# A wait of GpSimd for VectorE's bf16 operations in a transformer block whose order is written out

## The chip, the cores and the metric

The kernel runs on one core of a Trainium2 chip (trn2). A core has five engines that run their own instruction streams: TensorE (PE, matmuls into PSUM), VectorE (DVE), ScalarE (ACT), GpSimd (POOL) and SyncE (SP, which issues DMAs here). They share the on-chip memory SBUF and meet only at semaphores. The metric is the device time of one execution in microseconds; lower is better.

## The reference

One block of a transformer with adaptive normalization, in bf16, for 2048 tokens of width 640. `c` gives, through `silu(c) @ w_mod`, six rows of 640: shift, scale and gate for each half of the block.

```python
h = _layernorm(x) * (1 + ca) + sa
x = x + ga * _A_ref(h, A_wqkv, A_wo)      # attention
h = _layernorm(x) * (1 + cb) + sb
x = x + gb * _B_ref(h, ...)               # down(sigmoid(h @ w_gate) * (h @ w_up))
```

The attention has 32 heads of 20 channels. A token sees itself and the 255 tokens before it (a band of width 256): scores outside the band are masked, then softmax, the sum over values, and the projection `wo`. The feed-forward part has 1536 hidden channels.

## The kernel before, in words

The tokens go in 8 chunks of 256 (`CH`), a chunk as two blocks of 128 rows. Each chunk passes these stages:

- `ln1`, `ln_stats`: VectorE takes the statistics of each row (L766, L768), GpSimd adds the epsilon and raises to the power -0.5 (L771, L773), and VectorE, or for six blocks GpSimd, normalizes the row (`x<-x,st`: L786 on VectorE, L783 on GpSimd). The block is then transposed by TensorE or by a DMA (L793), and `modulate` applies scale and shift to each of its five tiles of 128 channels (L802; on VectorE, ScalarE or GpSimd).
- `qkv`: matmuls with `wqkv` (L679), evacuation from PSUM (L878 on VectorE).
- `attention`: two halves of four head groups. For each, `score_set` puts scores into PSUM (`S`, L680), ScalarE takes the exponential into a buffer `E` (L988), and GpSimd cuts the edges of the band with `affine_select` (`masks`, L1013: three masks for each group, two of 512 elements per row and one of 1024). Then a *burst* of 64 or 32 matmuls multiplies all four `E` with the values (`burst`, L680, `M<-E,V`); it waits for every mask of its half. `norm` transposes the result out of PSUM (L1057, `T<-M`), takes reciprocals (L1062), divides (L1064, `Tn<-T,Dr`) and transposes back (L1066), all on VectorE. DMAs carry the result through DRAM.
- `outproj`: matmuls with `wo` and the residual sum on VectorE (L1118), then the second normalization and modulation, into `h2T`.
- `mlp`: matmuls with `wg`, `wu` (L679), the gate by tanh on ScalarE (L1163) and a product on VectorE (L1165), the down projection with `wd`, the second residual sum (L1184), and the store.

The gates of the two halves are multiplied into the weights once: rows of `wo` (L1207) and `wd` (L1146). The twelve rows of `wd` are done ten on VectorE, two on GpSimd; the rows are 128 partitions by 640 bf16.

What sets the order is a list. Every operation of the program is made by `Prog.op`, and gets its place from `PRIO`, a list of 2126 numbers written out in the kernel: the number is the place in the order, and its remainder by 5 is the engine. `schedule` walks through the operations in that order and estimates a start time for each, from its dependencies, from its engine's last end (less a constant, `OVERLAP`) and from when a buffer comes free; with it, it chooses which buffer of a pool a tile gets. `emit` then writes each engine's stream, with semaphore waits for an operation's dependencies only. A wait that the engine has already made, or that a later count covers, is left out.

Some VectorE operations are marked `port=True`: normalization (L786), modulation (L802), the division (L1064), the gate multiplies (L1146, L1207) and two tiny ones (L731), 76 on VectorE in all. In `schedule`, a marked VectorE operation is taken to start after the GpSimd operation ahead of it, and a GpSimd operation after the marked VectorE operation ahead of it (`portend`). In the program before, no instruction enforces that: it is part of the estimate alone. `PORTLAG = 0.05` is defined in the kernel and not used there.

Of the kernel before, what the change touches and what calls it, by code (L numbers as in the profile page):

```python
# [81 lines left out]
class Prog:  # L82
# [70 lines left out]
    def schedule(self):  # L153


        free = {e: START for e in ENGS}
# [7 lines left out]
        portend = 0.0  # L164
# [3 lines left out]
        def slot_time(pool, s):  # L168
            ten = pool.tenant[s]
            if ten is None:  # L170
                if not all(x.done for x in pool.init[s]):
                    return None
                return max([x.end + x.lat for x in pool.init[s]], default=0.0)
            return None if ten.left else freed[ten]
# [4 lines left out]
        def reached(x):  # L179
            for lo, n, s, d in reversed(past):  # L180
                if lo < x:
                    return s + d * (x - lo) / n
            return -100.0

        def take(t, s):
            ten = t.pool.tenant[s]
            t.prev = list(t.pool.init[s]) if ten is None else list(ten.rel)
            t.slot = s
            t.pool.tenant[s] = t

        for o in sorted(self.ops, key=lambda x: x.prio):
            assert all(d.done for d in o.deps), o.tag
            e = ENGS[o.prio % 5]
            assert e in o.engs, (o.tag, e)
            o.eng = e
            st = max([o.tmin, free[e] + (SWITCH if e == "pe" and o.mode != pemode else 0.0)]
                     + [d.end + (0.0 if d.eng == "pe" and e == "pe" and d is not o.fence else d.lat) for d in o.deps])
            if o.isdma and e == "sp":
                st = max(st, bw - QMAX)
            for t in o.tiles:  # L200
                if t.slot is None:
                    step = 1 if t.mate is None else 2
                    best = None
                    for s in range(0, len(t.pool.tenant), step):
                        rts = [slot_time(t.pool, s + k) for k in range(step)]
                        if None not in rts and (best is None or max(rts) < best[0]):
                            best = (max(rts), s)
                    assert best is not None, (o.tag, t.name)
                    if t.mate is None:
                        take(t, best[1])  # L210
                    else:
                        take(t, best[1] + t.odd)
                        take(t.mate, best[1] + 1 - t.odd)
                for x in t.prev:
                    st = max(st, x.end + x.lat)
            if e == "dve" and o.port:
                st = max(st, free["pool"])
            elif e == "pool":
                st = max(st, portend)
                if o.part != part:  # L220
                    st = max(st, free[e] + OVERLAP[e] + 0.06)
                part = o.part
            dur = o.dur[e]
            if e == "pe":
                st = max(st, reached(count - RING) + FETCH, reached(count + o.ni - RING) + FETCH - dur)
                past.append((count, max(o.ni, 1), st, dur))
                count += max(o.ni, 1)
                pemode = o.mout
            o.start = st
            free[e] = st + dur - OVERLAP[e]  # L230
            if e == "dve" and o.port:
                portend = free[e]
            if o.isdma:
                turn = o.dlat > 3.0
                if e == "sp" and bw - st > 2.0:
                    free[e] += 0.35 if o.dur[e] > 1.0 else 0.1
                own = st + o.dlat + 2.0 * o.work
                bw = max(st + o.dlat, bw + (MIXED if turn != lastturn and bw > st + o.dlat else 0.0)) + o.work
                lastturn = turn
                o.end = max((own if e == "act" and own < bw else bw) - 0.83, st + dur)  # L240
                s = rr
                rr = (rr + 1) % NDMA
                dmacnt[s] += 16
                o.key, o.val = f"d{s}", dmacnt[s]
                if dmalast[s] is not None:
                    o.deps.append(dmalast[s])
                dmalast[s] = o
            else:
                o.end = st + dur
            order[e].append(o)  # L250
            o.done = True
            for t in o.tiles:
                t.left -= 1
                if t.left == 0:
                    last = {}
                    for x in t.ops:
                        if x.isdma:
                            last[x] = x
                    for e2 in ENGS:
                        xs = [x for x in t.ops if x.eng == e2 and not x.isdma]  # L260
                        if xs:
                            last[e2] = max(xs, key=lambda x: x.start)
                    t.rel = list(last.values())
                    freed[t] = max(x.end + x.lat for x in t.rel)
# [3 lines left out]
    def emit(self):  # L268
        nc = self.nc
        pos = {}  # L270
        for e in ENGS:
            for i, o in enumerate(self.order[e]):
                pos[o] = i
        need = {}
        for e in ENGS:
            for o in self.order[e]:
                ds = list(o.deps)
                for t in o.tiles:
                    ds.extend(t.prev)
                ws = []  # L280
                for d in ds:
                    if d is o:
                        continue
                    if d.eng == e and not d.isdma:
                        assert pos[d] < pos[o], (d.tag, o.tag)
                        if e in ("pe", "sp") and d is not o.fence:
                            continue
                    ws.append(d)
                    d.signal = True
                need[o] = ws  # L290
        for p, o in zip(self.order["pool"], self.order["pool"][1:]):
            if p.part != o.part and p not in need[o]:
                need[o].append(p)
                p.signal = True
        for e in ENGS:
            cnt = 0
            for o in self.order[e]:
                if o.isdma:
                    continue
                if o.signal:  # L300
                    cnt += 1
                    o.key, o.val = e, cnt
        handles = {}

        def h(k):
            if k not in handles:
                handles[k] = nc.alloc_semaphore(f"sem_{k}")
            return handles[k]

        finals = {}  # L310
        for o in self.order["sp"] + self.order["act"]:
            if o.isdma and o.tag == "out":
                finals[o.key] = max(finals.get(o.key, 0), o.val)
        with nc.Block() as block:
            for e in ENGS:
                ops = self.order[e]
                if not ops:
                    continue

                def body(engine, ops=ops, e=e):  # L320
                    seen = {}
                    for o in ops:
                        w = {}
                        for d in need[o]:
                            if seen.get(d.key, 0) < d.val and w.get(d.key, 0) < d.val:
                                w[d.key] = d.val
                        for k, v in w.items():
                            engine.wait_ge(h(k), v)
                            seen[k] = v
                        ins = o.fn(engine, e)  # L330
                        if o.isdma:
                            ins.then_inc(h(o.key), 16)
                        elif o.signal:
                            ins.then_inc(h(o.key), 1)
                    if e == "sp":
                        for k, v in finals.items():
                            if seen.get(k, 0) < v:
                                engine.wait_ge(h(k), v)

                getattr(block, ENGATTR[e])(body)  # L340
# [142 lines left out]
PORTLAG = 0.05  # L483
# [776 lines left out]
```

## Time and profile before

| what | value |
| --- | --- |
| time before, median of 3 runs | 329.09 us (328.69 to 329.17) |
| the profiled execution's own time | 329.38 us |
| its span in the profile | 327.6 us |
| granted TensorE clock | 1.00 |
| operations in the list: TensorE, ScalarE, VectorE, GpSimd, SyncE | 920, 331, 420, 255, 200 |

Times in the profile's views count from the start of the span. A row of a timeline gives the start, the length, the engine, the line of the kernel, the operation, the tiles it writes and reads (`out<-in`), the shapes, how many neighbouring operations are merged (`x4`), and in brackets the idle time of the engine ahead of it with what ended that time. A row of the waits gives the waiting engine, tile and line, then what it waited for, the sum in us, how often, and the longest. Engine busy time includes time in which an operation is held up after its start.

### The profile page before, as it was taken

The page shows a single profiled execution, that of the slowest core. Times are in us where ns is not written, and L with a number is a line of the kernel's source. Part 1 is how long each engine was busy: PE and PEld are TensorE (multiplying, and loading weights), DVE is VectorE, ACT ScalarE, POOL GpSimd, SP SyncE. Part 2 cuts the span into 40 slices and gives each one's busy share as a digit, 9 for nine tenths or more (in the row PEclk, how much of TensorE's full clock was granted, in tenths as well). Part 3 has the DMA queues.
Part 4 walks back from the last instruction along what each step waited for, and adds up shares of the span by engine and source line. Part 5 has one row for each costly group of instructions (what it writes and reads, how often), then busy time and mean ns, then how long its engine had stood idle before and what let it go on. Part 6 is the DMA issues. An engine that isn't in the chain of part 4 may idle for free.

```text
span 327.6 us, 11602 instructions
## 1 busy us (share of the span) xinstructions
PE 318.1 (97%) x4878; PEld 222.8 (68%) x4879; DVE 216.9 (66%) x420; ACT 216.3 (66%) x322; POOL 184.0 (56%) x267
## 2 busy tenths in 40 slices
PE   8899899999988999999999999999999999999997
PEld 3665555556765568766876467877787788877885
DVE  3799987898799894786575465746545576563332
ACT  2598787887756678977778886867679765112220
POOL 4228768868949495767385857573758383011000
PEclk9999999999999999999999999999999999999999
DMA  7989689779951339613422654320311003303001
GB/s 258 368 269 376 139 190 165 143 195 333 226 117 38 62 73 129 109 43 97 120 54 57 113 89 109 91 69 4 85 49 48 27 11 88 101 7 76 28 22 40
DMA packets 71038, 37.85 MB, mean 116 GB/s; under 512 B 45258, under 2 KB 69066, under 8 KB 70986
## 3 DMA queue, kind: packets, MB, share of 16 engines
q1 hardware_dynamic: 69680, 35.64, 45.2%
q10 hardware_dynamic: 1306, 1.48, 1.4%
q8 instruction: 38, 0.62, 0.8%
q14 instruction: 14, 0.11, 0.1%
HBM read 21.30 MB, written 5.25 MB: 81 GB/s over the span
## 4 chain that ended last, share of the span: by engine, by line
PE 83%; DVE 9%; issue 3%; ACT 1%; DMA 1%; POOL 1%; ACTq 0%; DVEq 0%
PE M L679 70%; PE S L680 7%; PE M L680 6%; DVE wd L1146 2%; DMA x<-in_A_x_dram 1%; DVE Tn L1064 1%; ACT E L988 1%; DVE stg L878 1%; DVE T L1057 1%; DVE x L786 1%; DVE h2T L802 1%; DVE On L1066 1%; POOL E L1013 1%; DVE st L766 1%; POOL st L773 0%
## 5 line engine op out<-in xcount | busy, mean ns | idle before, releaser
L1013 POOL TENSOR_SCALAR_AFFINE_SELECT E<-E 128x512 bf16<-128x512 bf16 (+1 forms) x176 | 143.8, 844 | 69.2 <-ACT E L988 66.6
L988 ACT ACTIVATE E<-S 128x512 bf16<-128x512 f32 (+2 forms) x184 | 150.2, 877 | 42.7 <-PE S L680 38.7
L679 PE MATMUL M<-wqkv,hT 128*128 128x480 bf16 (+1 forms) x340 | 71.5, 355 | 0.9 <-DVE hT L802 0.6
L679 PE MATMUL M<-h2T,wg 128*128 128x256 bf16 x480 | 64.4, 273 | 0.7 <-DVE h2T L802 0.7
L679 PE MATMUL M<-h2T,wu 128*128 128x256 bf16 x480 | 63.6, 273 | 1.1 <-DVE T L1057 1.1
L679 PE MATMUL M<-wd,hh 128*128 128x320 bf16 (+2 forms) x396 | 57.3, 295 | 1.5 <-DVE x L1118 1.2
L1165 DVE SCALAR_TENSOR_TENSOR hh<-sig,M 128x512 bf16<-128x512 f32 x48 | 32.0, 678 | 38.3 <-ACT sig L1163 29.1
L1163 ACT ACTIVATE sig<-M 128x512 f32<-128x512 f32 x48 | 28.7, 599 | 41.0 <-PE M L679 32.8
L679 PEld LDWEIGHTS M<-h2T,wg 128*128 128x128 bf16 x480 | 45.5, 98 | 8.6 <-DVE h2T L802 1.1
L679 PEld LDWEIGHTS M<-h2T,wu 128*128 128x128 bf16 x480 | 45.1, 98 | 8.7 <-DVE T L1057 1.4
L679 PEld LDWEIGHTS M<-wqkv,hT 128*128 128x128 bf16 x340 | 30.9, 98 | 28.2 <-issue 1.3
L679 PEld LDWEIGHTS M<-wd,hh 128*128 128x128 bf16 x396 | 37.0, 98 | 15.9 <-DVE x L1118 1.6
L1184 DVE TENSOR_TENSOR x<-M,x 128x320 bf16<-128x320 f32 (+2 forms) x33 | 15.3, 475 | 28.5 <-PE M L679 28.3
L680 PEld LDWEIGHTS S<-QT,KT 20*64 20x64 bf16 (+1 forms) x1856 | 20.0, 100 | 20.7 <-issue 9.4
L680 PE MATMUL S<-QT,KT 20*64 20x256 bf16 (+5 forms) x1856 | 32.3, 228 | 0.8 <-issue 0.8
L766 DVE BATCH_NORM_STATS2 st<-x 128x6 f32<-128x320 bf16 x64 | 28.7, 479 | 3.1 <-DMA x<-in_A_x_dram 2.7
L771 POOL TENSOR_SCALAR st<-st 128x2 f32<-128x2 f32 x16 | 3.9, 241 | 39.5 <-DVE st L768 39.3
L1057 DVE STREAM_TRANSPOSE T<-M 128x512 f32<-128x512 f32 x32 | 21.0, 693 | 6.7 <-PE M L680 6.5
L679 PE MATMUL M<-wo,oT 128*128 128x320 bf16 x160 | 24.9, 299 | 0.0
L680 PE MATMUL M<-E,V 128*32 128x128 bf16 (+1 forms) x960 | 22.8, 246 | 0.4 <-DVE shB L731 0.3
L680 PEld LDWEIGHTS M<-E,V 128*32 128x32 bf16 x960 | 19.0, 97 | 4.6 <-POOL E L1013 2.2
L786 DVE TENSOR_SCALAR x<-x,st 128x640 bf16<-128x640 bf16 x26 | 14.4, 581 | 9.9 <-POOL st L773 9.9
(75 smaller groups left out, 250.1 us busy)
## 6 DMA issues: line engine op xcount, KB each, us to landing
x<-in_A_x_dram SPq DMA_DIRECT2D x21, 160.0 KB, 3.9
doc<-On SPq DMA_DIRECT2D x64, 40.0 KB
wd<-in_B_w_down_dram SPq DMA_DIRECT2D x4, 480.0 KB, 5.6
out_dram<-x SPq DMA_DIRECT2D x11, 160.0 KB, 1.8
wd<-in_w_mod_dram SPq DMA_DIRECT2D x5, 320.0 KB
wqkv<-in_A_wqkv_dram SPq DMA_DIRECT2D x4, 400.0 KB, 7.5
wu<-in_w_mod_dram SPq DMA_DIRECT2D x5, 320.0 KB
oT<-doc SPq DMA_DIRECT2D x8, 192.0 KB, 2.4
```

Of the source, the lines that this page charges most:

```text
L679: return e.matmul(o, l, r, start=st, stop=sp, skip_group_check=True)
L680: return e.matmul(o, l, r, start=st, stop=sp, tile_position=tp, skip_group_check=True)
L766: A("dve", lambda e, g, bi=bi, j=j: e.bn_stats(v(bi * 12 + j * 6, 6), src[bi].ap[:, j * 320:(j + 1) * 320]), 0.48, reads=[src[bi].r()], wr ...
L771: A("pool", lambda e, g: e.tensor_scalar(v(28, n), var(), EPS, None, op0=ALU.add), 0.2, reads=[st.r(("m", bi)) for bi in range(n)], writes ...
L786: return e.tensor_scalar(dst[bi].ap[:], src[bi].ap[:], v(24 + 2 * bi, 1), v(30 + bi, 1), op0=ALU.subtract, op1=ALU.mult)
L988: A("act", lambda e, eng: e.activation(dst(), src(), ACT.Exp, scale=SM_SCALE), c_act(n), reads=[Sp.r()], writes=[E.r(key)], prio=3, tag=f" ...
L1013: A("pool", lambda e, eng: e.affine_select(rows(dst), rows(src), pattern=[[0, 8], [sign, n]], compare_op=ALU.is_ge, fill=0.0, base=base, c ...
L1057: A("dve", lambda e, g, h=h: e.transpose(T1.ap[:, 512 * h:512 * h + 512], X[h].ap), 0.694, reads=[X[h].r()], writes=[T1.r(h)], prio=3.5, t ...
L1146: A(WSE[1], lambda e, g, t=t: e.tensor_tensor(wd[:, t, :], wd[:, t, :], gbc[:], op=ALU.mult), WS, port=True, reads=[R_wd[t // 3], R_gbc], ...
L1163: A("act", lambda e, g, pg=pg, sg=sg: e.activation(sg.ap[:], pg.ap[:], ACT.Tanh, scale=0.5), c_act(512), reads=[pg.r()], writes=[sg.r()], ...
L1165: A("dve", lambda e, g, pu=pu, sg=sg, f0=f0: e.scalar_tensor_tensor(out=hh.ap[:, f0:f0 + 2, :], in0=sg.ap[:].rearrange("p (a b) -> p a b", ...
L1184: A("dve", lambda e, g, ps=ps, bi=bi, c0=c0, n=n: e.tensor_tensor(x1[bi].ap[:, c0:c0 + n], ps.ap[:, 0:n], x1[bi].ap[:, c0:c0 + n], op=ALU. ...
```

## The change

`emit` gets one more loop. It goes through VectorE's and GpSimd's operations together in planned order, remembers the last marked VectorE operation, and makes each GpSimd operation wait for that one's end. VectorE does not wait for GpSimd in return. In `schedule`, the estimate of when a GpSimd operation may start after a marked one becomes its end plus `PORTLAG`, where it was its end less `OVERLAP` (0.075 for VectorE). The list is the same, so order and engine of every operation are.

```diff
@@ schedule
             if e == "dve" and o.port:
-                portend = free[e]
+                portend = st + dur + PORTLAG
@@ emit
                     ws.append(d)
                     d.signal = True
                 need[o] = ws
+        held = None
+        for o in sorted(self.order["dve"] + self.order["pool"], key=lambda x: x.prio):
+            if o.eng == "dve":
+                held = o if o.port else held
+            elif held is not None:
+                need[o].append(held)
+                held.signal = True
         for p, o in zip(self.order["pool"], self.order["pool"][1:]):
```

## The prediction

> **What bounds the kernel now.** I read the page first, for the engine whose end is the end of the run.
>
> ```profile
> PE 318.1 (97%) x4878; PEld 222.8 (68%) x4879; DVE 216.9 (66%) x420; ACT 216.3 (66%) x322; POOL 184.0 (56%) x267
> ...
> PE 83%; DVE 9%; issue 3%; ACT 1%; DMA 1%; POOL 1%; ACTq 0%; DVEq 0%
> ```
>
> TensorE is busy 97% of 327.6 us and carries 83% of the chain that ended last; VectorE carries 9%, GpSimd 1%. The change moves GpSimd's start times. It can act on the end in two ways only: by VectorE operations that TensorE waits for, and by GpSimd results that come too late for TensorE. So the second view is TensorE's own waits (us in total, times, longest), and beside it one row of the view by windows, for the long second half (window, length, then busy time and count of PE and the other engines).
>
> ```profile
> PE M L679 <- DVE x L1118: 1.2, 1, 1.2
> PE M L679 <- DVE T L1057: 1.1, 1, 1.1
> PE M L679 <- DVE h2T L802: 0.7, 1, 0.7
> 104.00:276.00 172.00, 171.89 (x3016) 123.54 (x3015) 108.46 (x206) 130.77 (x189) 111.41 (x148) 1.00 0.35 74
> ```
>
> From 104 to 276 us TensorE is without work for 0.11 us: nothing can be gained there, only lost. What can be gained are three stalls of 1.2, 1.1 and 0.7 us, all of them on VectorE. Third, the views of single lines (count, then min/median/max in ns) for the operations that the change marks:
>
> ```profile
> L786 DVE TENSOR_SCALAR x<-x,st x26: 428/446/1215, 7.9 to 294.5; 128x640 bf16<-128x640 bf16 x26
> L802 DVE TENSOR_SCALAR h2T<-h2T,scB,shB x10: 334/374/1114, 75.3 to 214.7; 128x256 bf16<-128x256 bf16 x10
> L1064 DVE TENSOR_TENSOR Tn<-T,Dr x16: 812/825/1705, 30.7 to 277.6; 128x640 bf16<-128x640 f32 x16
> ```
>
> Each has a tight low value, which I take as its time alone (0.43, 0.33, 0.82 us), and a tail of two to three times that. The last view, the timelines of VectorE, GpSimd and TensorE around the three stalls, says where the tails lie; their rows stand with the steps below (start, length, engine, line, and in brackets the idle time before and what ended it).
>
> **The change, part by part.** It removes nothing and adds no arithmetic: a GpSimd operation starts only when the last marked VectorE operation ahead of it in the list has ended. Queued behind a waiting one are all later masks, statistics and modulations of GpSimd. The bursts (L680, M from E and V) wait for the masks, VectorE's normalizations for the statistics, TensorE's projections for the modulations. VectorE gets no new wait. By the list, 36 GpSimd operations get a wait on VectorE that they did not have. For the price of a handover the nearest row is one from VectorE to TensorE (75.25 + 2.22 = 77.47 to 77.53, rows below): 0.06, and I take 0.1. That is 3.6 us at most of the 143.6 us in which GpSimd is idle, and on the path only where a mask is the last thing a burst waits for. The changed line of the planner moves estimated starts by up to 0.125 us; order and engine come from the list, so only the choice among free buffers could change. I take nothing for it.
>
> *Around 70 us, a loss.*
>
> ```profile
> 67.22 0.67 POOL L1013 TENSOR_SCALAR_AFFINE_SELECT E<-E 128x512 bf16<-128x512 bf16 x1
> 68.20 2.40 POOL L1013 TENSOR_SCALAR_AFFINE_SELECT E<-E 128x1024 bf16<-128x1024 bf16 x3 [0.31 <-ACT E L988]
> 67.29 0.77 DVE L786 TENSOR_SCALAR x<-x,st 128x640 bf16<-128x640 bf16 x1 [0.38 <-POOL st L773]
> 70.18 1.50 PE L680 MATMUL M<-E,V 128*32 128x128 bf16 x64
> ```
>
> The mask at 67.22 stands behind the normalization of 67.29 in the list. That one then takes 0.43 instead of 0.77 and ends at 67.72; the mask runs from 67.8 to 68.45, and the masks of 68.20, of which the burst needs the first two, start 0.25 late. The burst has no other cover, so it starts 0.25 late: +0.25. Bounds: 0, if the masks absorb it, and 0.6, if the normalization is not shortened (68.06 + 0.1 + 0.67, against 68.20).
>
> *Around 77 us, a gain.*
>
> ```profile
> 75.25 2.22 DVE L802 TENSOR_SCALAR h2T<-h2T,scB,shB 128x256 bf16<-128x256 bf16 x4
> 76.28 1.12 POOL L1013 TENSOR_SCALAR_AFFINE_SELECT E<-E 128x1024 bf16<-128x1024 bf16 x1 [0.41 <-ACT E L988]
> 77.53 1.05 PE L679 MATMUL M<-h2T,wg 128*128 128x256 bf16 x8 [0.67 <-DVE h2T L802]
> ```
>
> The last of the four modulations is the one of 1.11 us (the maximum above): it meets the mask of 76.28, which stands behind it in the list. With the mask held it takes 0.33, so the four end at 75.25 + 0.25 + 2.22 - 0.78 = 76.94. TensorE, ready at 77.53 - 0.67 = 76.86 and itself 0.25 later now, does not stall: -0.67. GpSimd starts that mask 0.75 late; it is back on time by the next gap that ScalarE makes.
>
> *Around 91 us, a gain.*
>
> ```profile
> 86.07 5.05 DVE L1146 TENSOR_TENSOR wd<-wd,gbc 128x640 bf16<-128x640 bf16 x4
> 91.04 1.30 DVE L1057 STREAM_TRANSPOSE T<-M 128x512 f32<-128x512 f32 x2
> 92.27 1.37 DVE L1146 TENSOR_TENSOR wd<-wd,gbc 128x640 bf16<-128x640 bf16 x3
> 87.54 3.23 POOL L1146 TENSOR_TENSOR wd<-wd,gbc 128x640 bf16<-128x640 bf16 x2
> 87.62 1.50 PE L680 MATMUL M<-E,V 128*32 128x128 bf16 x64
> ...
> 91.80 1.49 PE L679 MATMUL M<-h2T,wu 128*128 128x256 bf16 x12 [1.12 <-DVE T L1057]
> ```
>
> Here one operation is seen in both conditions: four rows of `wd` in 5.05 us (1.26 each) while GpSimd does two of its own, and three in 1.37 us (0.46 each) afterwards. GpSimd's two stand in the list behind VectorE's fourth and seventh. With them held, VectorE's second still waits for the mask that ends where GpSimd's row of 87.54 starts (it is ahead in the list); then the second, third and fourth take 0.46 each and end at 88.9 instead of 91.1. The transposes then wait for the end of the burst, 87.62 + 1.50 = 89.12, and the first of the two (0.65) is done at 89.8. TensorE's stalled matmuls need that one and were ready at 91.80 - 1.12 = 90.68: -1.12. If the transposes followed 0.9 later than this, the gain would begin to shrink. GpSimd's multiplies come some us later than now; what needs them, TensorE's down projections (M from wd), of which the row of 102.14 below is one, comes later still.
>
> *Around 102 us, a gain.*
>
> ```profile
> 97.10 1.70 DVE L1146 TENSOR_TENSOR wd<-wd,gbc 128x640 bf16<-128x640 bf16 x2
> 98.72 1.71 DVE L1064 TENSOR_TENSOR Tn<-T,Dr 128x640 bf16<-128x640 f32 x1
> 100.46 1.25 DVE L1066 STREAM_TRANSPOSE On<-Tn 128x1024 bf16<-128x1024 bf16 x1
> 101.63 1.05 DVE L1118 TENSOR_TENSOR x<-M,x 128x320 bf16<-128x320 f32 x2
> 96.51 5.04 POOL L1013 TENSOR_SCALAR_AFFINE_SELECT E<-E 128x1024 bf16<-128x1024 bf16 x5 [4.26 <-ACT E L988]
> ...
> 103.29 3.36 POOL L1013 TENSOR_SCALAR_AFFINE_SELECT E<-E 128x512 bf16<-128x512 bf16 x4 [0.57 <-ACT E L988]
> 102.14 2.94 PE L679 MATMUL M<-wd,hh 128*128 128x320 bf16 x20 [1.24 <-DVE x L1118]
> ...
> 109.67 1.50 PE L680 MATMUL M<-E,V 128*32 128x128 bf16 x64
> ```
>
> GpSimd's masks from 96.51 run into two multiplies (1.70 instead of 0.92) and the division (1.71 instead of 0.82), and these hold up the residual sum of 101.63, for which TensorE stalls 1.24. All of these masks stand behind the division in the list. Held, they leave VectorE 0.78 + 0.89 = 1.67 us shorter, more than the 1.24: -1.24. The cost is GpSimd's. In the new time, 1.54 us earlier after the steps above, the division ends at 100.43 - 1.54 - 1.67 = 97.2; GpSimd's work up to the burst is the two rows, 8.40 us, and two short operations between them of about 1.2 together, from which about as much comes off when nothing collides: by this estimate it ends at 105.6. The burst, 2.8 us earlier than 109.67, wants it at 106.8. What hides the delay is 1.2 us of slack; if that is gone, each further us is paid by TensorE.
>
> *From 104 us on.* VectorE's collisions are gone there too, but TensorE does not wait for them. The largest single delay is this one:
>
> ```profile
> 241.36 0.56 POOL L802 TENSOR_SCALAR h2T<-h2T,scB,shB 128x256 bf16<-128x256 bf16 x1
> 246.81 8.98 POOL L1013 TENSOR_SCALAR_AFFINE_SELECT E<-E 128x1024 bf16<-128x1024 bf16 x11 [4.89 <-ACT E L988]
> 244.73 0.82 DVE L1064 TENSOR_TENSOR Tn<-T,Dr 128x640 bf16<-128x640 f32 x1
> ```
>
> The modulation and a mask ahead of it (0.66, the short kind) now wait for the division until 245.6 and end at 246.8, where the next mask starts in any case: the 4.89 us of idle hide it, just. I take +0.1 for the whole stretch, with bounds of 0 and 0.9 (the price of the modulations in the slower rival).
>
> The sum: 0.25 - 0.67 - 1.12 - 1.24 + 0.1 = -2.7 us. The profiled execution took 329.38 us, 0.3 above the median of 329.09; I carry the difference over to the median: 326.4 us.
>
> The Trainium skill, page "SBUF — State Buffer", section "Who interferes with whom", describes the port pair shared by the two engines as an exclusive lock, held for a whole instruction by whoever starts first while the other blocks. The tails agree with the blocking. By that rule alone a collision is paid once in either order, so that the change would only swap who pays, for a time of 329.1; that is the exchange rival.
>
> **The rivals.** *Part of it comes back.* The masks for the burst of 109.67 have 1.2 us of slack by my count. If the division ends at 98.4 instead of 97.2 it is used up, and with 1.2 more the third gain is gone: 327.6 us. For it: ten operations with hardly a gap (0.57). Against: they too get shorter when nothing collides.
>
> *Exchange.* What VectorE gains GpSimd loses, and the bursts lose with it: 329.1 us. For it: one engine's work is only put behind the other's. Against: TensorE's waits name VectorE three times and GpSimd never, and GpSimd is idle for 44% of the span. A wait that is always satisfied when it is reached would give the same time; against that stands every tail above.
>
> *Slower: GpSimd is pushed and VectorE not relieved.* If the 1.26 us at 86.07 were VectorE's own, the division would end at 100.43 as now. The masks of 96.51 would start 4.0 us late, 3.4 after the gap of 0.57, end 3.4 after 106.65 and miss the burst of 109.67 by 0.4; the burst of 70.18 would lose 0.6; and the lateness would reach the next modulations:
>
> ```profile
> 116.60 1.16 POOL L802 TENSOR_SCALAR h2T<-h2T,scB,shB 128x256 bf16<-128x256 bf16 x2
> 118.41 0.66 DVE L802 TENSOR_SCALAR h2T<-h2T,scB,shB 128x256 bf16<-128x256 bf16 x1
> 118.62 1.11 PE L679 MATMUL M<-h2T,wg 128*128 128x256 bf16 x8
> ```
>
> GpSimd's second would follow VectorE's (119.07) and end at 119.7; TensorE wants it some 0.2 us into its row of 118.62, and so loses 0.9. Together 1.9 us: 331.0 us. It decides if VectorE's fourth row of `wd` still ends after 90.7. Against it: the 0.46 us at 92.27.
>
> **How the numbers follow.** Forecast 62%, partial return 15%, exchange 10%, slower 13%. The forecast's own range is 325.4 (1 us more, if smaller collisions also give something) to 327.5 (the first and the last step at their upper bounds, 0.35 and 0.8 more). Forecast and partial return hold 77%, so the range has to reach the exchange: 325.4 to 329.2 us. About 0.2% (0.66 us) is what a measurement of this kernel tells from no change: faster 0.77, same 0.10, slower 0.13.
>
> **What would show it.** Right: rows of `wd` on VectorE at 0.43 to 0.5 us but for the one behind a mask, the division at 98.72 down to 0.82, no wait of TensorE above 0.2 us on L1057, L1118 or L802, and idle time of GpSimd put down to VectorE's L1064 and L1146. Wrong: TensorE waiting for L1013 ahead of bursts (partial return or exchange), rows of `wd` still above 1 us (slower), or TensorE waiting for GpSimd's L802 near 116 us.

## The result, and the profile after

The changed kernel takes 324.79 us (median of 4, 324.43 to 325.56) against 329.13 us (328.69 to 329.41) for the kernel before, a ratio of 0.9873 (95% interval 0.9852 to 0.9894). The profiled execution took 324.87 us with a span of 323.1. The forecast was 326.4 us, the range 325.4 to 329.2: faster, as said, by 4.3 us instead of 2.7, and so below the range. Line numbers of the changed kernel are 7 higher than before behind the added loop in `emit` (L679 is L686, L1013 is L1020, L1064 is L1071).

The page after, its busy times and the shares of the chain that ended last:

```profile
PE 317.6 (98%) x4879; PEld 223.5 (69%) x4879; DVE 210.0 (65%) x420; ACT 216.1 (67%) x322; POOL 177.3 (55%) x267
...
PE 90%; DVE 3%; DMA 2%; POOL 2%; issue 2%; ACT 1%; DVEq 0%; POOLq 0%
```

VectorE's share of the chain went from 9% to 3%. Both VectorE (216.9 to 210.0) and GpSimd (184.0 to 177.3) are busy 7 us less, with the same operations: what went is time in which started operations stood still. The waits after, all of TensorE's that the view lists, and the three largest new ones of GpSimd:

```profile
PE S L666 <- DVE E L661: 1.3, 1, 1.3
PE M L686 <- DVE hT L809: 0.6, 1, 0.6
PE M L687 <- DVE shB L738: 0.3, 1, 0.3
PE M L686 <- DVE stg L885: 0.3, 1, 0.3
PE M L686 <- ACT hT L808: 0.2, 1, 0.2
PE M L687 <- POOL E L1020: 0.2, 1, 0.2
...
POOL E L1020 <- DVE Tn L1071: 22.5, 7, 4.7
POOL E L1020 <- DVE x L793: 6.4, 6, 2.6
POOL wd L1153 <- DVE wd L1153: 3.0, 2, 1.6
```

The stalls of 1.2, 1.1 and 0.7 us on VectorE's L1118, L1057 and L802 are gone, and TensorE waits for a mask once, 0.2 us. GpSimd's idle time now names the division and `wd`, as forecast. The timelines of VectorE, GpSimd and TensorE of the changed kernel around the three places:

```profile
66.50 0.45 DVE L793 TENSOR_SCALAR x<-x,st 128x640 bf16<-128x640 bf16 x1 [0.38 <-POOL st L780]
74.71 1.17 DVE L809 TENSOR_SCALAR h2T<-h2T,scB,shB 128x256 bf16<-128x256 bf16 x4
84.69 2.89 DVE L1153 TENSOR_TENSOR wd<-wd,gbc 128x640 bf16<-128x640 bf16 x4
89.03 1.39 DVE L1153 TENSOR_TENSOR wd<-wd,gbc 128x640 bf16<-128x640 bf16 x3
95.34 0.82 DVE L1071 TENSOR_TENSOR Tn<-T,Dr 128x640 bf16<-128x640 f32 x1
...
67.09 2.50 POOL L1020 TENSOR_SCALAR_AFFINE_SELECT E<-E 128x512 bf16<-128x512 bf16 x3 [0.62 <-DVE x L793]
76.01 1.09 POOL L1020 TENSOR_SCALAR_AFFINE_SELECT E<-E 128x1024 bf16<-128x1024 bf16 x1 [0.98 <-DVE h2T L809]
90.57 1.40 POOL L1153 TENSOR_TENSOR wd<-wd,gbc 128x640 bf16<-128x640 bf16 x1 [1.42 <-DVE wd L1153]
96.32 3.96 POOL L1020 TENSOR_SCALAR_AFFINE_SELECT E<-E 128x1024 bf16<-128x1024 bf16 x5 [2.42 <-DVE Tn L1071]
100.78 3.97 POOL L1020 TENSOR_SCALAR_AFFINE_SELECT E<-E 128x512 bf16<-128x512 bf16 x5
...
69.64 1.50 PE L687 MATMUL M<-E,V 128*32 128x128 bf16 x64 [0.18 <-POOL E L1020]
74.92 1.19 PE L686 MATMUL M<-wqkv,hT 128*128 128x480 bf16 x5
75.94 1.25 PE L686 MATMUL M<-h2T,wg 128*128 128x256 bf16 x10
86.24 1.50 PE L687 MATMUL M<-E,V 128*32 128x128 bf16 x64
88.03 1.27 PE L686 MATMUL M<-h2T,wg 128*128 128x256 bf16 x10
89.13 1.47 PE L686 MATMUL M<-h2T,wu 128*128 128x256 bf16 x12
97.79 0.43 PE L687 MATMUL S<-QT,KT 20*64 20x256 bf16 x24
98.15 2.89 PE L686 MATMUL M<-wd,hh 128*128 128x320 bf16 x20
105.63 1.50 PE L687 MATMUL M<-E,V 128*32 128x128 bf16 x64
```

The four rows of `wd` take 2.89 us instead of 5.05 (one behind a mask at 1.37, three at 0.49 to 0.54), the division 0.82 instead of 1.71, the four modulations 1.17 instead of 2.22. Where the time went is read from the starts of TensorE's rows, the same row in both profiles:

| row of TensorE | start before | start after | earlier by | step |
| --- | --- | --- | --- | --- |
| `wqkv`, ahead of the burst | 69.06 | 68.27 | 0.79 | |
| burst | 70.18 | 69.64 | 0.54 | +0.25 |
| burst | 87.62 | 86.24 | 1.38 | -0.84 |
| `wu`, stalled on L1057 | 91.80 | 89.13 | 2.67 | -1.29 |
| `wd`, stalled on L1118 | 102.14 | 98.15 | 3.99 | -1.32 |
| burst | 109.67 | 105.63 | 4.04 | -0.05 |
| `wu` near 119 us | 119.68 | 115.33 | 4.35 | -0.31 |
| `wu` near 273 us | 272.93 | 268.44 | 4.49 | -0.14 |

The last row's 4.49 is the whole difference of the spans (327.6 to 323.1). The changed execution was 0.79 us ahead before the burst of 70 us, which then lost 0.25. The early lead comes mainly from a place that no marked operation explains. TensorE before, then after:

```profile
40.40 0.22 PE L680 MATMUL S<-QT,KT 20*64 20x64 bf16 x4 [0.77 <-issue]
40.56 1.79 PE L679 MATMUL M<-wqkv,hT 128*128 128x480 bf16 x8
```

```profile
39.29 2.00 PE L686 MATMUL M<-wqkv,hT 128*128 128x480 bf16 x9
```

The 0.77 us stand against "issue", no engine. The lead here is 1.27 us, of which 0.48 is gone again by 46 us, so that 0.79 is left. So two things were open: does the change take that gap away, and do the steps behind 70 us belong to the three places that the forecast named?

### The profile page after: what moved, and what is told of

It is laid out like the page before. It is cut to its first block, busy times and chain, and to the rows that moved or that the text cites. A ratio compares the mean times of both kernels' runs of the same rounds, so it can differ in the third digit from the quotient of the medians.

```text
span 323.1 us, 11621 instructions
## 1 busy us (share of the span) xinstructions
PE 317.6 (98%) x4879; PEld 223.5 (69%) x4879; DVE 210.0 (65%) x420; ACT 216.1 (67%) x322; POOL 177.3 (55%) x267
## 4 chain that ended last, share of the span: by engine, by line
PE 90%; DVE 3%; DMA 2%; POOL 2%; issue 2%; ACT 1%; DVEq 0%; POOLq 0%
PE M L686 73%; PE S L687 7%; PE M L687 6%; PE S L666 2%; POOL E L1020 1%; DMA gbc<-gate 1%; DMA gate<-gq 1%; PE S L686 1%; ACT E L995 0%; POOL st L780 0%; DVE hh L1172 0%; DVE x L793 0%; DVE stg L885 0%; DVE KT L885 0%; DVE wo L1214 0%
## 5 line engine op out<-in xcount | busy, mean ns | idle before, releaser
L1020 POOL TENSOR_SCALAR_AFFINE_SELECT E<-E 128x512 bf16<-128x512 bf16 (+1 forms) x176 | 138.8, 818 | 67.2 <-ACT E L995 30.1
L686 PE MATMUL M<-wqkv,hT 128*128 128x480 bf16 (+1 forms) x340 | 71.5, 355 | 0.9 <-DVE hT L809 0.6
L686 PE MATMUL M<-h2T,wg 128*128 128x256 bf16 x480 | 64.1, 273 | 0.0
L686 PE MATMUL M<-h2T,wu 128*128 128x256 bf16 x480 | 63.5, 273 | 0.0
L686 PE MATMUL M<-wd,hh 128*128 128x320 bf16 (+2 forms) x396 | 57.2, 295 | 0.2
L686 PEld LDWEIGHTS M<-h2T,wg 128*128 128x128 bf16 x480 | 45.8, 98 | 7.4 <-issue 0.2
L686 PEld LDWEIGHTS M<-wqkv,hT 128*128 128x128 bf16 x340 | 30.8, 98 | 28.4 <-DMA wqkv<-in_A_wqkv_dram 0.9
L686 PEld LDWEIGHTS M<-h2T,wu 128*128 128x128 bf16 x480 | 45.4, 98 | 6.8 <-issue 0.2
L686 PEld LDWEIGHTS M<-wd,hh 128*128 128x128 bf16 x396 | 37.1, 98 | 14.5 <-DVE hh L1172 0.9
L1064 DVE STREAM_TRANSPOSE T<-M 128x512 f32<-128x512 f32 x32 | 21.1, 694 | 7.2 <-PE M L687 7.1
L686 PE MATMUL M<-wo,oT 128*128 128x320 bf16 x160 | 24.9, 299 | 0.0
L1125 DVE TENSOR_TENSOR x<-M,x 128x320 bf16<-128x320 f32 x32 | 15.5, 486 | 8.3 <-PE M L686 7.7
```

The costliest lines, as they stand in the source:

```text
L686: return e.matmul(o, l, r, start=st, stop=sp, skip_group_check=True)
L1020: A("pool", lambda e, eng: e.affine_select(rows(dst), rows(src), pattern=[[0, 8], [sign, n]], compare_op=ALU.is_ge, fill=0.0, base=base, c ...
L1064: A("dve", lambda e, g, h=h: e.transpose(T1.ap[:, 512 * h:512 * h + 512], X[h].ap), 0.694, reads=[X[h].r()], writes=[T1.r(h)], prio=3.5, t ...
L1125: A("dve", lambda e, g, ps=ps, bi=bi, half=half: e.tensor_tensor(x1[bi].ap[:, half * 320:half * 320 + 320], ps.ap[:, 0:320], x1[bi].ap[:, ...
```

## The experiments

With the planner's line alone, every engine's operations are those of the kernel before, in order and buffers; so the waits are what there is to divide. All kernels but the two repeats change the added loop, each in one line but for the one with waits both ways, and each ratio is against the kernel before, run beside it.

**The waits by stretches of the list.** Before place 2400 (about 67 us), from 2400 to 3800 (to about 106 us), and from 3800 on.

```diff
-            elif held is not None:
+            elif held is not None and o.prio < 2400:
```

> Only the GpSimd operations at places below 2400 in the list (to about 66 us) wait. Against the kernel before, TensorE in the changed kernel was 0.9 us ahead at 46 us and had lost nothing up to 69 us. Theory A (the waits themselves shift the DMAs around 30 to 36 us, and with them a stall of 0.77 us that the profile before shows as 'issue' at 39.6): this kernel shows no such stall and takes 328.3 us. Rival B (that stall came or went by chance of one execution): the time is within 0.3 of 329.1.

328.72 us, ratio 0.9998 (0.9981 to 1.0016). The early waits alone bring nothing that can be measured.

```diff
-            elif held is not None:
+            elif held is not None and 2400 <= o.prio < 3800:
```

> Only the operations from place 2400 to 3800 (about 67 to 106 us) wait: the stretch with the three stalls. Theory A (three stalls on VectorE go, one burst is late): +0.33 - 0.84 - 1.30 - 1.32 = -3.1, 326.0 us. Rival C (the late masks of this stretch are paid for unless the waits after it hold VectorE's collisions down): 327 us or more, with TensorE later than in the changed kernel at 118 us.

325.66 us, ratio 0.9908 (0.9888 to 0.9928). TensorE's starts step by +0.26, -0.83, -1.30 and -1.32 at the burst and the three stalls: the steps of the table. Its profile is also 1.17 us ahead by 41 us, though up to there it has no wait that the kernel before lacks.

```diff
-            elif held is not None:
+            elif held is not None and o.prio >= 3800:
```

> Only the operations from place 3800 on (from about 107 us) wait. Theory A: small gains where VectorE's results were just in time for TensorE (around 119 us), 0.3 to 0.5 us, 328.7 us. Rival C: nothing is gained there and late masks cost something, 329.1 to 329.9 us.

328.16 us, ratio 0.997 (0.9954 to 0.9985). The three stalls stay, the small steps are there (-0.13, -0.18, -0.16). In this stretch the forecast had +0.1. The three parts sum to -0.02, -0.92 and -0.30%, together -1.24%, which is the whole change's -1.27% within the intervals: they add up.

**The early gap.** Some 9 us ahead of the gap of 0.77 us, GpSimd's normalization at place 1153 gets a wait: it starts at 29.36 us before and at 31.65 after.

```diff
-            elif held is not None:
+            elif held is not None and o.prio != 1153:
```

> The changed kernel without one wait: GpSimd's normalization at place 1153, whose block SyncE transposes next, doesn't wait for the division ahead of it. Theory A (this wait is the one that moves the DMAs): the transpose at 30 us is early again, the stall of 0.8 us on 'issue' at 39 us is back, and the time is 325.6 to 325.8 us. Rival B: it is that of the changed kernel, 324.8 us.

325.42 us, ratio 0.9901 (0.9881 to 0.9922), and no gap came back. So the theory that this wait removes the gap has fallen. The two kernels again, unchanged, the changed one first:

> The changed kernel once more, beside many runs of the one before. From the traces, the waits account for +0.33 - 0.84 - 1.30 - 1.32 - 0.5 = -3.6 us; the first profile showed 0.9 us more, gained before 41 us. Theory A (that part varies from execution to execution and isn't the change's): the paired difference is -3.3 to -3.9 us, and this profile stands elsewhere than 39.3 us at the projection that the first one began there. Rival B (it belongs to the change): -4.3 to -4.8 us.

> The kernel before once more, for a second profile of it. Theory A (the stall of 0.77 us on 'issue' at 39.6 us is one execution's): the stall is absent or of another length, TensorE begins the same projection between 39.4 and 40.6 us, and the three stalls on VectorE at 77.5, 91.8 and 102.1 us are there unchanged within 0.1. Rival B: the stall of 0.77 is there again.

The changed kernel: 325.19 us, ratio 0.9882 (0.9863 to 0.9902), span 323.1. The kernel before: 329.15 us, ratio 1.0015 (0.9991 to 1.0039), span 326.9. This second profile of the kernel before has no 0.77, while its three stalls are the same:

```profile
PE M L679 <- DVE x L1118: 1.2, 1, 1.2
PE M L679 <- DVE T L1057: 1.1, 1, 1.1
PE M L679 <- DVE h2T L802: 0.7, 1, 0.7
```

So the early gap is one execution's and not the kernel's. Between the two repeats the spans differ by 3.8 us, and the steps behind 67 us give 3.7 of it (+0.25, -0.82, -1.30, -1.32, -0.17, -0.22, -0.13).

**The first two stalls, then the third.**

```diff
-            elif held is not None:
+            elif held is not None and 2800 <= o.prio < 3420:
```

> Only places 2800 to 3420 wait: GpSimd's two rows of wd, the mask and statistics ahead of them and the masks just behind. Theory A (each stall is its own collision): the stall at 91 us goes and, since the mask of 76.3 us stands in this stretch too, that of 77 us with it; the one of 102 us stays: -0.84 - 1.30, 327.0 us. Rival D (the stall at 102 us comes from the lateness that the rows of wd left on VectorE): it goes as well, 325.7 us.

327.82 us, ratio 0.9965 (0.9944 to 0.9986). TensorE's waits in this kernel:

```profile
PE M L686 <- DVE x L1125: 1.4, 1, 1.4
...
PE M L686 <- DVE stg L885: 0.8, 1, 0.8
```

The first two stalls go (-0.78 and -1.26), the third stays at 1.4. The profile also lost 0.90 us at 45.7 us, the wait for `stg`, and the first wait that this kernel adds lies behind 67 us: variation again. The median came out above what was expected; the interval (0.5 to 1.8 us gained) holds the 1.84 of the steps (0.78 + 1.26, less the 0.20 by which the third stall's row came later) at its very edge. Why the third stall grew stays open.

```diff
-            elif held is not None:
+            elif held is not None and 3420 <= o.prio < 3800:
```

> Only places 3420 to 3800 wait: the masks that collide with two rows of wd and the division at 97 to 100 us. Theory A: only the stall at 102 us goes, 1.3 us, 327.8 us. The masks begin at the division's end, which without the earlier gains is 98.8, and have 1.1 us less room before their burst; rival C (the room is too small): the burst is late by up to 0.5 us and the time 328.3 us.

327.46 us, ratio 0.9944 (0.9923 to 0.9965). Only the third goes, -1.31, and the burst behind it is not late:

```profile
PE M L686 <- DVE T L1064: 1.1, 1, 1.1
PE M L686 <- DVE h2T L809: 0.7, 1, 0.7
```

So the first two stalls, taken together, and the third hang on the waits of their own stretch, and neither gain needs the other's waits.

**How much waiting is right.** One wait less, one direction more, and all of VectorE's operations in place of the marked ones.

```diff
-            elif held is not None:
+            elif held is not None and held.prio != 2402:
```

> The changed kernel without the waits for the normalization at place 2402 (66.5 us): the one place where the change made a burst late. Theory A: the mask starts with the normalization again, that takes 0.77 us instead of 0.45, and the burst at 69.6 us is 0.28 to 0.33 earlier against what is ahead of it; nothing else moves: 0.3 us less than the changed kernel, 324.7 us beside its 325.0. Rival C (the later normalization delays the modulations at 75 us): the gain there shrinks by as much, and the time is that of the changed kernel.

324.68 us, ratio 0.985 (0.98 to 0.9899). Without the wait behind the normalization near 67 us, the +0.25 at the burst of 70 us is gone, and the gains stay (-0.83, -1.30, -1.32, -0.17, -0.18, -0.16). By the trace this is the best version; by the time, 0.1 to 0.5 us below the change, it is not told apart from it.

```diff
+        ahead = None
         for o in sorted(...):
+            if o.eng == "pool":
+                ahead = o
+            elif o.port and ahead is not None:
+                need[o].append(ahead)
+                ahead.signal = True
```

> The changed kernel, in which also each marked VectorE operation waits for the GpSimd operation ahead of it in the list. Theory A (the two engines block each other anyway once one has started, and the gain is that GpSimd's operations no longer start first): nothing is left to save, and VectorE now waits for GpSimd operations that haven't started because ScalarE is late; TensorE's waits on VectorE come back, 326 to 329 us. Rival E (a collision stretches both operations beyond their sum, so that full separation is better still): 324.0 us or less.

326.99 us, ratio 0.9917 (0.9892 to 0.9943): VectorE waiting for GpSimd as well gives about 2 us of the gain back. TensorE's waits, in which L1026 is the mask and L815 the modulation:

```profile
PE M L693 <- POOL E L1026: 0.9, 3, 0.4
PE M L692 <- POOL h2T L815: 0.4, 1, 0.4
```

The masks now come late for three bursts, and the steps are +0.38 near 70 us, +0.40 near 88, +0.49 near 119 and +0.33 near 190. The time lies where Theory A put it, but not for its reason: the three stalls on VectorE do not come back. What is lost is lost to GpSimd's late results.

```diff
-                held = o if o.port else held
+                held = o
```

> Each GpSimd operation waits for the last VectorE operation ahead of it in the list, marked or not. VectorE's transposes, evacuations and statistics are then waited for too, 0.2 to 1.25 us each. Theory A (the masks have about 0.9 us of room before the burst near 105.7 us, and less elsewhere): TensorE waits for masks before several bursts, the gain shrinks by 1 to 4 us: 326 to 329 us. Rival F (GpSimd's idle time covers any wait of this size): 324.8 to 325.3 us.

367.30 us, ratio 1.1138 (1.1083 to 1.1194). The direction was expected, the size not by far: the expectation was a gain smaller by 1 to 4 us, and thirteen waits for masks alone take 26.4 us.

```profile
PE M L687 <- POOL E L1020: 26.4, 13, 4.7
POOL E L1020 <- DVE On L1073: 21.9, 7, 6.5
```

GpSimd now follows VectorE through the transposes of L1073 (beside one of these and the residual sums, the ten masks of 96.32 and 100.78 above run without a tail), and so through VectorE's own waits for TensorE; the masks miss their bursts by up to 4.7 us. Part of the rest of the 42.6 us by which its span (365.7) is longer than the changed kernel's is a lower clock behind the longest waits, shown in the last section. What helps is not that GpSimd waits, but what it waits for.

## Where the forecast held, and where it failed

**The mechanism held, in its order.** The rows of `wd` (but for the one behind a mask), the division and the modulations came down to about their times alone, the three stalls went, and no new wait above 0.2 us came. The masks ahead of the burst near 107 us end at 100.78 + 3.97 = 104.75 and the burst starts at 105.63: 0.9 us of slack, where 1.2 was estimated. The burst near 70 us loses 0.25, as the sum had it. Partial return did not happen. The slower rival's condition, that the fourth row of `wd` still ends after 90.7, was not met: it ends at 84.69 + 2.89 = 87.58, in the old time 88.96 (with the 1.38 by which the burst of 87.62 is earlier), where 88.9 was worked out.

**Failed: the step that sized the three stalls.** The forecast took -0.67, -1.12 and -1.24 from the idle column; TensorE's starts moved by -0.84, -1.29 and -1.32, 0.42 us more in sum. The rows above show what the idle column leaves out. After the change the row of 74.92 lasts to 76.11, and the next starts at 75.94: with nothing waited for, this row's shown end lies 0.17 us behind the start of the next. So an idle time of 0.67 is a loss of 0.67 + 0.17 = 0.84. The same overlap is 0.17 at 88.03 (ends 89.30, next 89.13) and 0.07 at 97.79 (98.22, 98.15), which gives 1.29 and 1.31. All three agree with the steps to 0.01 us. The same overlap stands in the profile before, where the row of 75.46 lasts to 76.65 and the next starts at 76.48, so this could have been read there:

```profile
75.46 1.19 PE L679 MATMUL M<-wqkv,hT 128*128 128x480 bf16 x5
76.48 0.38 PE L679 MATMUL M<-h2T,wg 128*128 128x256 bf16 x2
```

**Failed: "nothing can be gained" from 104 us on.** The stretch was put at +0.1 and gave about -0.5. The sentence took the 0.11 us of idle time for all there was to gain; by the same overlap, waits below 0.17 us show no idle time at all. Near 273 us, TensorE before, then after:

```profile
272.57 0.38 PE L679 MATMUL M<-h2T,wg 128*128 128x256 bf16 x2
272.93 0.61 PE L679 MATMUL M<-h2T,wu 128*128 128x256 bf16 x4
```

```profile
268.22 0.38 PE L686 MATMUL M<-h2T,wg 128*128 128x256 bf16 x2
268.44 0.60 PE L686 MATMUL M<-h2T,wu 128*128 128x256 bf16 x4
```

The same two rows of 0.38 us, 0.36 from start to start before and 0.22 after: a wait of 0.14 without an idle time. Near 119 us the cause can be followed. VectorE and GpSimd before, then after:

```profile
114.83 0.83 DVE L1064 TENSOR_TENSOR Tn<-T,Dr 128x640 bf16<-128x640 f32 x1
115.57 1.22 DVE L786 TENSOR_SCALAR x<-x,st 128x640 bf16<-128x640 bf16 x1
...
114.83 1.78 POOL L1013 TENSOR_SCALAR_AFFINE_SELECT E<-E 128x1024 bf16<-128x1024 bf16 x1 [1.85 <-ACT E L988]
```

```profile
110.78 0.82 DVE L1071 TENSOR_TENSOR Tn<-T,Dr 128x640 bf16<-128x640 f32 x1
111.52 0.44 DVE L793 TENSOR_SCALAR x<-x,st 128x640 bf16<-128x640 bf16 x1
...
112.09 1.09 POOL L1020 TENSOR_SCALAR_AFFINE_SELECT E<-E 128x1024 bf16<-128x1024 bf16 x1 [2.55 <-DVE x L793]
```

Before, the mask starts with the division and takes 0.69 us longer than alone; the normalization starts in the mask's rest and takes 0.78 longer. Each pays for the one that came first. After, the mask starts 0.13 us behind the normalization's end, and all three take their time alone. The modulation and the casts behind this normalization come earlier by the 0.78, and TensorE's rows of 118.62 and 119.68 lose their small waits. That this moves those rows, and not another of the waits from place 3800 on, was argued from the order of the rows; that it is those waits together was shown by the run that has them alone.

**The exchange rival was half right.** At this place, with TensorE's lead of 4.04 us taken off, VectorE's normalization ends 0.79 us earlier and GpSimd's mask 0.61 us later: an exchange indeed. Its second half, that the bursts lose with GpSimd, did not come: TensorE waited for VectorE, and for GpSimd it had slack. Here the row bears out what the Trainium skill says on the page "SBUF — State Buffer", section "Who interferes with whom": the one that comes second blocks, and the order of issue decides who. By the trace it is nearly a full block: 0.69 of the 0.83 us that the division lasted, 0.78 of the 1.04 us that the mask still had.

**The sum of the two.** With 0.42 us more at the stalls and about 0.6 us more behind them, the forecast of 326.4 us becomes 325.4: the lower end of the range, which had allowed 1 us for smaller collisions alone. The measured 324.79 lies 0.6 us below that. No run shows an added wait that brings these 0.6 us: the early waits alone bring nothing that can be measured, and the steps behind 67 us are all counted.

**Small terms.** A handover from VectorE to GpSimd was put at 0.1; it is 67.09 - 66.95 = 0.14 behind the normalization, 0.13 behind the modulations (75.88 to 76.01) and 0.16 behind the division (96.16 to 96.32).

**What stays open.** The steps behind 67 us give 3.7 us in both pairs of profiles. The medians differ by 4.3 us, with an interval of 3.5 to 4.9, and in the repeat by 3.8 (325.19 against 328.97, the runs of the kernel before that stand beside it). Whether the early waits add some tenths to the 3.7 was not settled: alone they gave 0.9998, which leaves up to 0.6 us either way. The early part of a profile varies by as much (last section), so that the first measurement fell 0.6 us below the range's end can be chance. The first two stalls were not parted from each other, and a kernel in which only VectorE waits was not run.

## What to carry to other kernels

Size a wait by the distance from start to start of the same rows where they run without it, not by the idle column: here 0.07 to 0.17 us of each wait were hidden, and waits below that did not show at all. Where two engines hold each other up, look whom the bound engine waits for, and let that engine go first; one-sided waits, on the operations that really collide, brought 1.3%, waits both ways gave half of the gain back, and waits on every operation cost 11%. Before a difference between two profiles is put down to a change, look at it in a second profile of the same kernel: the gap of 0.77 us that this change seemed to take away stood in one execution of the kernel before and not in the next.

## What the runs showed of the hardware

The first 41 us vary from one execution to the next with the same instructions: the projection that starts at 40.56 in the first profile of the kernel before starts at 39.80 in the second, and at 39.29 and 39.68 in the two of the changed kernel.

A long wait of TensorE costs more than its length. In the kernel that waits for all of VectorE, a wait of 4.66 us stands ahead of a burst, the 64 matmuls of which take 2.75 us instead of 1.50. Its timeline, and two windows (length, busy times, and as the last but two the granted clock):

```profile
254.47 2.75 PE L687 MATMUL M<-E,V 128*32 128x128 bf16 x64 [4.66 <-POOL E L1020]
```

```profile
254.00:257.00 3.00, 2.53 (x64) 2.02 (x64) 0.00 (x0) 0.00 (x0) 0.41 (x1) 0.50 0.00 0
257.00:261.00 4.00, 4.00 (x49) 2.27 (x45) 2.38 (x5) 2.42 (x3) 0.66 (x1) 0.66 0.00 0
```

The granted clock is 0.50 in the first and 0.66 on average in the second. In the same profile a stretch at 0.50 goes with each of the other waits above 3.8 us (3.81, 3.86 and 4.24), while waits of up to 2.12 us leave the clock at 1.00. That agrees with the page "TensorE: Matmul & The Clock Gate" of the Trainium skill, section "HAM oscillation — how this bites in real kernels", by which gaps of more than about 3.4 us bring the clock down to half.
